# Attention and a silu MLP in one kernel: two vector operations one unit later, and a third of a cast moved to GpSimd

## The chip, the cores and the metric

The kernel runs on one core of a Trainium2 chip. The metric is device time in microseconds of one execution, the median of the runs. All engines of the core work from instruction streams of their own and meet through semaphores: TensorE (PE, with PEld for its weight loads), VectorE (DVE), ScalarE (ACT), GpSimd (POOL), and SyncE (SP), which here issues DMAs.

## The reference

An efficient attention over 8 batches, 8 heads, 576 positions and head dimension 64 gives 4608 tokens of 512 features, and a two-layer MLP with silu follows. Cut to what matters:

```python
def attn(q, k, v):                      # each 8 x 8 x 576 x 64, float32
    q_s = softmax(q, axis=-1)
    k_s = softmax(k, axis=2)            # over the positions
    kv = einsum('bhsd,bhse->bhde', k_s, v)
    return einsum('bhsd,bhde->bhse', q_s, kv)

x = attn(q, k, v).transpose(0, 2, 1, 3).reshape(4608, 512)
h = x @ w_in                            # 512 x 2048
out = (h * sigmoid(h)) @ w_out          # 2048 x 512, float32 out
```

## The kernel before, in words

**Attention, batch by batch.** For a batch, `load` brings q, k and v in two halves each (two pairs of heads, the argument `cc`), in float32, with two buffers for each of the three names. ScalarE takes the exponentials into bf16 (`exp_q`, L108; `exp_k`, L113). VectorE sums q's exponentials (`qsum`, L154 or in two pieces L156, and its reciprocal L158), and `qnorm` (L163) multiplies by it, on VectorE or GpSimd. `vcast` (L91 on VectorE and GpSimd, L89 on ScalarE, both in the helper `copy`) casts v to bf16 into `vaug`, beside a column of constants that gives the sum over k. `kv` (L195) is the small product of k and v, `kvcopy` (L206, L208) its division into `kvn`. The transposed q (by TensorE, L181, for batches 0 and 1, by a DMA transpose, L173, after) times `kvn` gives the tokens: `xt_mm` (L234), whose result is copied to the tile `XT`.

**The MLP, in chunks of tokens.** Chunk 0 is batch 0's 576 tokens; the later ones have 512 columns, the next of them 448 that are new. The first product of chunk 0 runs block by block of 128 features (`wide_mm`, L267; silu as ScalarE's tanh, L256, and VectorE's product, L257). Its second product is plain (`mm2_plain`, L414). From chunk 1 on the products follow a scheme with seven products instead of eight (orders 1, 2, 6, 5, 7, 4, 3). In the first layer, `group` (L377) makes one of the seven: products 1, 6 and 7 are copied from PSUM to `h` (`group_snap`, L89 or L91), and after products 2, 7 and 3 VectorE adds the bank to `h` (`group_add`, L355). The bank of products 2, 5 and 3 is one and the same, so TensorE can't start product 5 before the addition after 2 has read it, nor 3 before the one after 7. Silu reads PSUM or `h` (`group_silu`, L361). The scheme's sums and differences of weights and tokens are VectorE's: `ws_op` (L328), `xs_op` (L338), `t_op` (L461) and, for the second layer, `s_op` (L451). The second layer's products are `prod` (L477); its results are scaled and added by VectorE (L497, L508, and L725 at the end) and stored. Half of chunk 1's first layer is done without the scheme (`mm1`, L285).

**The order of work** is written out by hand: each engine runs its instructions in the order in which the program emits them. The program keeps a list of units, each a group of matmuls with what follows them, and `plan(u, f)` hangs other work in front of unit `u`:

```python
for u, f in enumerate(units):
    for g in at.get(u, ()):
        g()
    f()
```

`begin[1]`, called `b1`, is where the first product of chunk 1 is interleaved with the second of chunk 0. Units b1+0 to b1+8 are plain second products, b1+9 is product 1 of the group, b1+10 plain, b1+11 product 2 with its addition, b1+12 product 6, b1+13 plain, b1+14 product 5. `begin[NCH]` is the unit at which the last chunk's second layer begins; in the 28 units before it the last chunk's first layer alternates with the second layer of the chunk before. There, `s_op(last, 1, 4, 8)` and `s_op(last, 2, 4, 8)` prepare half of two operands of the last chunk's second layer.

**The start.** It isn't in units but emitted in line. SP issues the loads of batch 0 (q, q, k, v, k, v). GpSimd makes a copy of one element that waits for k's first half (`gate`, L569), and issues then, in this order, five loads of `w_in` (L554, cast from float32 to fp16 on the way) and the loads of batch 1 between those of `w_out` (L560): q, q, w_out, k, k, w_out, v, v. TensorE runs fillers on a constant tile (`heat`, L551) where it would stand still: three of them lie before the second `kv` of batch 0. The second cast of v of batch 0 is done in two parts, one pair's head on ScalarE and the other on VectorE.

Of the kernel before, what the change touches and what calls it, by code (L numbers as in the profile page):

```python
# [17 lines left out]
def kernel(  # L18
# [9 lines left out]
    nc = tc.nc  # L28
    B, H, S, D = q.shape
# [3 lines left out]
    J = S // P  # L33
# [7 lines left out]
    NCH = NT // TCH  # L41
# [25 lines left out]
    vaug = glob.tile([128, J, NG, E1], BF16, name="vaug")  # L67
# [19 lines left out]
    def copy(eng, o, i):  # L87
        if eng is nc.scalar:
            eng.copy(out=o, in_=i)  # L89
        else:  # L90
            eng.tensor_copy(o, i)  # L91

    def load(b, name, src, cc, eng):
        t = ld.tile([128, 2, J * D], FP32, name=name)
        st[b][name, cc] = t
        x = src[b].rearrange("(g r) (p j) d -> g (r p) (j d)", r=2, j=J)
        eng.dma_start(out=t, in_=x.rearrange("g x y -> x g y")[:, 2 * cc:2 * cc + 2, :])

    def jgd(b, name, cc):
        return st[b][name, cc].rearrange("p g (j d) -> p j g d", d=D)  # L100

    def half(t, cc):
        return t[:, :, cc * 128:(cc + 1) * 128].rearrange("p j (g d) -> p j g d", d=D)

    def exp_q(b, cc, g0=0, g1=2):
        if "eq" not in st[b]:
            st[b]["eq"] = ap.tile([128, J, NG * D], BF16, name="eq")
        nc.scalar.activation(  # L108
            out=half(st[b]["eq"], cc)[:, :, g0:g1], in_=jgd(b, "qt", cc)[:, :, g0:g1], func=ACT.Exp
        )  # L110
# [1 line left out]
    def exp_k(b, cc):  # L112
        nc.scalar.activation(out=half(ek, cc), in_=jgd(b, "kt", cc), func=ACT.Exp)  # L113

    def vcast(b, cc, eng, g0=0, g1=2):
        o = vaug[:, :, 2 * cc + g0:2 * cc + g1, 0:D]
        i = jgd(b, "vt", cc)[:, :, g0:g1, :]
        copy(eng, o, i)

    def vcast_at(t, b, cc):  # L120

        if t == 2 and cc == 1:
            nc.gpsimd.tensor_copy(gate, SS[2][0:1, 0, 0:1])
        vcast(b, cc, nc.gpsimd)
# [20 lines left out]
    def new_zq(b):  # L145
        if "zq" not in st[b]:
            st[b]["zq"] = ap.tile([128, 2, J, 2], FP32, name="zq", bufs=2)
            st[b]["rzq"] = ap.tile([128, 2, J, 2], FP32, name="rzq", bufs=2)

    def qsum(b, cc, gs=None):  # L150
        new_zq(b)
        z, e = st[b]["zq"][:, cc], half(st[b]["eq"], cc)
        if gs is None:
            nc.vector.reduce_sum(out=z, in_=e, axis=AX.X)  # L154
        else:
            nc.vector.reduce_sum(out=z[:, :, gs], in_=e[:, :, gs, :], axis=AX.X)  # L156
        if gs != 0:
            nc.vector.reciprocal(out=st[b]["rzq"][:, cc], in_=z)  # L158

    def qnorm(b, cc, eng):  # L160
        e = half(st[b]["eq"], cc)
        r = st[b]["rzq"][:, cc]
        eng.tensor_tensor(  # L163
            out=e, in0=e, in1=r[:, :, :, None].to_broadcast([128, J, 2, D]), op=ALU.mult
        )
# [21 lines left out]
    def trcopy(b, cc, j0, j1, bank, eng=nc.vector):  # L187
        t = PS[:, bank, :].bitcast(BF16)[:, 0:(j1 - j0) * 128].rearrange("x (j y) -> x j y", y=128)
        copy(eng, new_qt(b)[:, j0:j1, cc, :], t)
# [249 lines left out]
    def blk(t, kh, th):  # L439
        return GTS[t % 2][:, kh * HF:(kh + 1) * HF, th * HT:(th + 1) * HT]  # L440

    def s_op(t, i, f0=0, f1=HF):
        in0, in1, op = {
            1: (blk(t, 0, 1), blk(t, 1, 1), ALU.add),
            2: (SS[1], blk(t, 0, 0), ALU.subtract),
            3: (blk(t, 0, 0), blk(t, 0, 1), ALU.subtract),
            4: (blk(t, 1, 0), SS[2], ALU.subtract),
        }[i]
        f = slice(f0, f1)
        o = blk(t, 0, 1) if i == 3 else SS[i]  # L450
        nc.vector.tensor_tensor(out=o[:, f], in0=in0[:, f], in1=in1[:, f], op=op)  # L451
# [97 lines left out]
    def heat(n, bank=5):  # L549
        for _ in range(n):  # L550
            nc.tensor.matmul(out=PS[:, bank, :], lhsT=warm[:, 0:128], rhs=warm, start=True, stop=True)  # L551

    def load_w1(f0, f1, c0=0, c1=NC):
        nc.gpsimd.dma_start(  # L554
            out=W1[:, c0:c1, f0 * 128:f1 * 128],
            in_=w_in[c0 * 128:c1 * 128, f0 * 128:f1 * 128].rearrange("(c p) f -> p c f", p=128),
        )
# [14 lines left out]
    load_w1(4, 8)  # L572
    load_w1(8, 12)
    load_w1(12, 16)
    load(1, "qt", q, 0, nc.gpsimd)
    load(1, "qt", q, 1, nc.gpsimd)
    load_w2(0, 4)
# [11 lines left out]
    heat(7)  # L589
    qnorm(0, 1, nc.vector)  # L590
    vcast(0, 0, nc.scalar)
    trcopy(0, 0, 0, 5, 0, nc.scalar)
    trcopy(0, 0, 5, J, 1)
# [5 lines left out]
    xt_mm(0, 0, 0, 320, 4, 0)  # L599
    xt_mm(0, 0, 320, 256, 0, 0)  # L600
    heat(3, 6)
    vcast(0, 1, nc.scalar, 0, 1)
    vcast(0, 1, nc.vector, 1, 2)
    trcopy(0, 1, 0, 5, 2, nc.scalar)
    trcopy(0, 1, 5, J, 3)
    kv(0, 1)
# [16 lines left out]
    def plan(u, f):  # L623
        at.setdefault(u, []).append(f)
# [7 lines left out]
    begin = {1: len(units)}  # L632
# [83 lines left out]
    begin[NCH] = len(units)  # L716
    last = NCH - 1
    plan(begin[NCH] - 11, lambda: s_op(last, 1, 4, 8))
    plan(begin[NCH] - 7, lambda: s_op(last, 2, 4, 8))
    plan(begin[NCH], lambda: (s_op(last, 1, 0, 4), s_op(last, 2, 0, 4), s_op(last, 3)))  # L720
    plan(begin[NCH] + 6, lambda: s_op(last, 4))

# [48 lines left out]
    b1 = begin[1]  # L771
# [26 lines left out]
    plan(b1 + 10, lambda: (xs_op(1, 1), ws_op(1, 0)))  # L798
    plan(b1 + 10, lambda: (xs_op(1, 2), xs_op(1, 3), xs_op(1, 4)))
    plan(b1 + 10, lambda: exp_q(2, 0))  # L800
    plan(b1 + 11, lambda: (qsum(2, 0, 0), qsum(2, 0, 1), qnorm(2, 0, nc.gpsimd)))
    plan(b1 + 13, lambda: exp_q(2, 1))
    plan(b1 + 14, lambda: exp_k(2, 0))
    plan(b1 + 14, lambda: (qsum(2, 1, 0), qsum(2, 1, 1), qnorm(2, 1, nc.gpsimd)))
# [56 lines left out]
```

## Time and profile before

| | |
|---|---|
| median of 11 runs | 263.33 us |
| lowest and highest | 263.04 and 264.27 us |
| the profiled execution | 263.6 us |
| its span in the profile | 261.8 us |
| TensorE busy | 252.2 us, 96% of the span |
| VectorE, ScalarE, GpSimd busy | 209.0, 187.5 and 65.6 us |
| granted TensorE clock, mean | 0.995 |

The profile is of one execution. The span runs from the first to the last instruction of the program; the execution's own time has 1.8 us more around it. All times in the timelines below count from the span's start. Matmuls are pipelined and their ends are modelled, so a matmul's duration is longer than the distance to the next one. A line number stands for the line in the kernel that made the instruction; the helper `copy` gives its own two lines to everything that goes through it. In the chain of work, each step is followed back to what released it.

### The profile page before, as it was taken

To read this page: it belongs to the slowest core of one execution; us is meant where nothing else is said; L and a number is where in the kernel's file an instruction comes from. 1 tells how busy PE (TensorE), PEld (TensorE's weight loads), DVE (VectorE), ACT (ScalarE), POOL (GpSimd) and SP (SyncE) were. 2 spreads that over 40 slices of the span, in tenths; PEclk is the share of its full clock that TensorE was granted. 3 is DMA by queue.
4 is the path that set the end of the run, shared out by engine and by line. 5 is a ranking of instruction groups with operands and counts; after the bars stand their busy time and mean duration, and the time that the engine had idled before them with its cause. 6 is when DMAs were issued, how large, how long until landed. Compare 5 with 4: busy or idle time off the path is not lost.

```text
span 261.8 us, 6409 instructions
## 1 busy us (share of the span) xinstructions
PE 252.2 (96%) x2732; PEld 203.5 (78%) x2732; DVE 209.0 (80%) x268; ACT 187.5 (72%) x212; POOL 65.6 (25%) x63
## 2 busy tenths in 40 slices
PE   8899899799999999999999999999999999999992
PEld 2467656465888888888888888888888888888881
DVE  2867797998997999799979997999798548855832
ACT  4766987798995799579957995799573748484610
POOL 1653791470360306030603060306000000000003
PEclk9999999999999999999999999999999999999997
DMA  7999999669999586957794879540534003300624
GB/s 238 345 185 296 299 314 334 262 106 377 318 341 199 165 221 231 202 145 199 253 223 122 213 241 195 149 92 3 90 75 87 3 0 81 81 3 1 139 64 120
DMA packets 35964, 45.89 MB, mean 175 GB/s; under 512 B 16208, under 2 KB 21008, under 8 KB 35936
## 3 DMA queue, kind: packets, MB, share of 16 engines
q1 hardware_dynamic: 29568, 33.69, 47.5%
q0 software_dynamic: 6128, 11.60, 17.3%
q8 instruction: 21, 0.34, 0.5%
q10 hardware_dynamic: 240, 0.20, 0.2%
q14 instruction: 7, 0.06, 0.1%
HBM read 36.70 MB, written 9.44 MB: 176 GB/s over the span
## 4 chain that ended last, share of the span: by engine, by line
PE 83%; DMA 5%; issue 4%; POOL 2%; ACT 2%; DVE 2%; POOLq 0%; ACTq 0%
PE PS L477 36%; PE PS L377 34%; DMA qt<-in_q_dram 5%; PE PS L414 5%; PE PS L285 2%; PE PS L234 2%; PE PS L195 2%; POOL W L554 1%; PE PS L267 1%; POOL out_dram L740 1%; ACT eq L108 1%; DVE zq L156 1%; ACT sg L256 0%; PE PS L181 0%; DVE h L355 0%
## 5 line engine op out<-in xcount | busy, mean ns | idle before, releaser
L355 DVE TENSOR_TENSOR h<-PS,h 128x1024 f32<-128x1024 f32 (+1 forms) x45 | 53.9, 1198 | 12.2 <-ACT h L89 6.3
L477 PEld LDWEIGHTS <-GT 128*128 128x128 f16 x512 | 49.6, 98 | 6.9 <-issue 1.2
L377 PEld LDWEIGHTS <-WS 128*128 128x128 f16 x480 | 46.8, 98 | 7.9 <-issue 2.3
L477 PE MATMUL PS<-W,GT 128*128 128x256 f16 x384 | 49.1, 273 | 0.0
L377 PE MATMUL PS<-XS,WS 128*128 128x256 f16 (+1 forms) x360 | 46.3, 272 | 1.5 <-DVE h L355 1.5
L361 ACT ACTIVATE GT<-h 128x1024 f16<-128x1024 f32 (+1 forms) x45 | 46.1, 1047 | 0.3 <-DVE h L355 0.3
L89 ACT COPY h<-PS 128x1024 f32<-128x1024 f32 (+1 forms) x35 | 35.1, 1004 | 14.8 <-PE PS L377 14.2
L477 PEld LDWEIGHTS <-S 128*128 128x128 f16 x384 | 37.2, 98 | 5.2 <-issue 1.0
L163 POOL TENSOR_TENSOR eq<-eq,rzq 128x1152 bf16<-128x1152 bf16 x13 | 27.5, 2117 | 54.6 <-DVE rzq L158 51.8
L377 PEld LDWEIGHTS <-W 128*128 128x128 f16 x360 | 34.7, 98 | 4.7 <-issue 0.2
L477 PE MATMUL PS<-T,S 128*128 128x256 f16 x256 | 32.7, 273 | 0.0
L377 PE MATMUL PS<-XT,W 128*128 128x256 f16 (+1 forms) x240 | 29.5, 272 | 0.0
L361 ACT ACTIVATE GT<-PS 128x1024 f16<-128x1024 f32 (+1 forms) x15 | 15.3, 1017 | 18.9 <-PE PS L377 18.9
L91 POOL CAST vaug<-vt 128x1152 bf16<-128x1152 f32 x12 | 14.8, 1242 | 45.2 <-DMA vt<-in_v_dram 45.2
L108 ACT ACTIVATE eq<-qt 128x1152 bf16<-128x1152 f32 (+1 forms) x18 | 19.1, 1059 | 3.5 <-DMA qt<-in_q_dram 3.5
L740 POOL DMA_DIRECT2D out_dram<-ow x5 | 2.7, 546 | 72.5 <-DVE ow L725 72.5
L154 DVE TENSOR_REDUCE zq<-eq 128x18 f32<-128x1152 bf16 x12 | 16.1, 1345 | 4.0 <-ACT eq L108 4.0
L113 ACT ACTIVATE ek<-kt 128x1152 bf16<-128x1152 f32 x16 | 18.4, 1154 | 1.3 <-DMA kt<-in_k_dram 1.3
L267 PE MATMUL PS<-XT,W 128*128 128x288 f16 x128 | 16.0, 286 | 0.8 <-DVE GT L257 0.8
L477 PE MATMUL PS<-W,S 128*128 128x256 f16 x128 | 16.5, 273 | 0.0
L497 DVE SCALAR_TENSOR_TENSOR ow<-PS,sc 128x512 f32<-128x512 f32 x7 | 4.8, 691 | 14.5 <-ACT sc L493 14.5
L267 PEld LDWEIGHTS <-W 128*128 128x128 f16 x128 | 12.4, 98 | 4.3 <-issue 1.2
(79 smaller groups left out, 348.9 us busy)
## 6 DMA issues: line engine op xcount, KB each, us to landing
out_dram<-ow SPq DMA_DIRECT2D x64, 128.0 KB, 2.4
qt<-in_q_dram SPq DMA_DIRECT2D x12, 576.0 KB, 4.7
kt<-in_k_dram SPq DMA_DIRECT2D x12, 576.0 KB, 5.4
vt<-in_v_dram SPq DMA_DIRECT2D x12, 576.0 KB, 6.0
qt<-in_q_dram POOLq DMA_DIRECT2D x4, 576.0 KB, 10.5
kt<-in_k_dram POOLq DMA_DIRECT2D x4, 576.0 KB, 13.6
vt<-in_v_dram POOLq DMA_DIRECT2D x4, 576.0 KB, 12.7
W<-in_moe_w_out_dram POOLq DMA_DIRECT2D x4, 512.0 KB, 14.9
```

What stands on the lines that cost most here:

```text
L89: eng.copy(out=o, in_=i)
L91: eng.tensor_copy(o, i)
L108: nc.scalar.activation(out=half(st[b]["eq"], cc)[:, :, g0:g1], in_=jgd(b, "qt", cc)[:, :, g0:g1], func=ACT.Exp)
L113: nc.scalar.activation(out=half(ek, cc), in_=jgd(b, "kt", cc), func=ACT.Exp)
L154: nc.vector.reduce_sum(out=z, in_=e, axis=AX.X)
L163: eng.tensor_tensor(out=e, in0=e, in1=r[:, :, :, None].to_broadcast([128, J, 2, D]), op=ALU.mult)
L267: nc.tensor.matmul(out=PS[:, WIDE[fb] + n, 0:S // 2], lhsT=W1[:, c, fb * 128:(fb + 1) * 128], rhs=XTS[0][:, c, n * (S // 2):(n + 1) * (S / ...
L355: nc.vector.tensor_tensor(out=four(t, i), in0=group_bank(t, True), in1=four(t, i), op=ALU.add)
L361: nc.scalar.activation(out=group_out(t, f, n), in_=x, func=ACT.Silu, scale=1.0 / XS)
L377: nc.tensor.matmul(out=PS[:, bank + p // 2, (p % 2) * HT:(p % 2) * HT + width(t)], lhsT=a[:, c, p * 128:(p + 1) * 128], rhs=bb[:, c, 0:wid ...
L414: nc.tensor.matmul(out=PS[:, 2 + tb, :], lhsT=GTS[t % 2][:, fc, tb * 128:(tb + 1) * 128], rhs=W2[:, fc, :], start=(fc == 0), stop=(fc == N ...
L477: nc.tensor.matmul(out=PS[:, bank, m * HN:(m + 1) * HN], lhsT=a[:, fc, m * 128:(m + 1) * 128], rhs=bb[:, fc, :], start=(first and fc == 0) ...
```

## The change

Three edits:

- `plan` for the sum of batch 2's first half of q, with its reciprocal and `qnorm`, goes from unit b1+11 to b1+12. On VectorE the addition after product 2 now stands ahead of the sum instead of behind the reciprocal. `qnorm` keeps its place on GpSimd.
- `plan` for `s_op(last, 2, 4, 8)` goes from seven units before `begin[NCH]` to six. On VectorE one addition (L355) now stands ahead of it.
- In the second cast of v of batch 0, the rows of tokens `j` 6 to 8 of both heads go to GpSimd, and ScalarE and VectorE keep rows 0 to 5. On GpSimd, the cast stands behind the five loads of `w_in` and ahead of the loads of batch 1 and `w_out`. TensorE's `kv` waits for it at row 6.

Nothing else changes its order on any engine, and no DMA is added.

```diff
-    def vcast(b, cc, eng, g0=0, g1=2):
-        o = vaug[:, :, 2 * cc + g0:2 * cc + g1, 0:D]
-        i = jgd(b, "vt", cc)[:, :, g0:g1, :]
+    def vcast(b, cc, eng, g0=0, g1=2, j0=0, j1=J):
+        o = vaug[:, j0:j1, 2 * cc + g0:2 * cc + g1, 0:D]
+        i = jgd(b, "vt", cc)[:, j0:j1, g0:g1, :]
         copy(eng, o, i)
...
     load_w1(12, 16)
+    vcast(0, 1, nc.gpsimd, 0, 2, 6, J)
     load(1, "qt", q, 0, nc.gpsimd)
...
     heat(3, 6)
-    vcast(0, 1, nc.scalar, 0, 1)
-    vcast(0, 1, nc.vector, 1, 2)
+    vcast(0, 1, nc.scalar, 0, 1, 0, 6)
+    vcast(0, 1, nc.vector, 1, 2, 0, 6)
...
-    plan(begin[NCH] - 7, lambda: s_op(last, 2, 4, 8))
+    plan(begin[NCH] - 6, lambda: s_op(last, 2, 4, 8))
...
-    plan(b1 + 11, lambda: (qsum(2, 0, 0), qsum(2, 0, 1), qnorm(2, 0, nc.gpsimd)))
+    plan(b1 + 12, lambda: (qsum(2, 0, 0), qsum(2, 0, 1), qnorm(2, 0, nc.gpsimd)))
```

## The prediction

> **What bounds the kernel now.** I read the page first: its busy shares and its chain, for which engine sets the end.
>
> ```profile
> PE 252.2 (96%) x2732; PEld 203.5 (78%) x2732; DVE 209.0 (80%) x268; ACT 187.5 (72%) x212; POOL 65.6 (25%) x63
> ...
> PE 83%; DMA 5%; issue 4%; POOL 2%; ACT 2%; DVE 2%; POOLq 0%; ACTq 0%
> ```
>
> TensorE is busy for 96% and is 83% of the chain. A change pays only where TensorE stands still, so the next view is the list of waits, for TensorE's rows.
>
> ```profile
> PE PS L377 <- DVE h L355: 1.5, 1, 1.5
> ...
> PE PS L267 <- DVE GT L257: 0.8, 1, 0.8
> ```
>
> Two waits matter: 1.5 us on an addition (L355) and 0.8 us on a silu product (L257). I looked up each in the timeline. First the stretch around 46 us (start, duration, instruction; in brackets idle time and what ended it):
>
> ```profile
> 44.10 0.93 PE L377 MATMUL PS<-XT,W 128*128 128x224 f16 x8
> ...
> 45.49 1.41 DVE L156 TENSOR_REDUCE zq<-eq 128x9 f32<-128x576 bf16 x2 [0.98 <-ACT eq L108]
> 45.63 1.03 PE L414 MATMUL PS<-W,GT 128*128 128x512 f16 x4
> ...
> 46.94 0.27 DVE L158 RECIPROCAL rzq<-zq 128x18 f32<-128x18 f32 x1
> 47.12 1.03 DVE L355 TENSOR_TENSOR h<-PS,h 128x896 f32<-128x896 f32 x1
> 47.39 2.11 POOL L163 TENSOR_TENSOR eq<-eq,rzq 128x1152 bf16<-128x1152 bf16 x1 [7.26 <-DVE rzq L158]
> ...
> 48.06 1.98 DVE L328 TENSOR_TENSOR WS<-WS,W 128x1024 f16<-128x1024 f16 x1
> 48.20 0.93 PE L377 MATMUL PS<-XS,WS 128*128 128x224 f16 x8 [1.54 <-DVE h L355]
> ```
>
> The addition's product was ready at 45.03 (44.10 + 0.93). VectorE stood idle then, but its next instruction in order was the sum of batch 2's exponentials (L156), which waited for ScalarE until 45.49. Sum and reciprocal take 1.6 us, and so the addition starts at 47.12 and TensorE resumes at 48.20.
>
> The other wait comes from the start. The chain holds "DMA qt" from 12.59 to 25.74; ScalarE's first exponential of batch 1 waits for it and pushes silu and TensorE:
>
> ```profile
> 12.59 1.48 POOL L97 DMA_DIRECT2D qt<-in_q_dram  x2
> ...
> 25.76 0.68 ACT L108 ACTIVATE eq<-qt 128x576 bf16<-128x576 f32 x1 [0.82 <-DMA qt<-in_q_dram]
> ...
> 28.94 3.10 PE L267 MATMUL PS<-XT,W 128*128 128x288 f16 x24 [0.76 <-DVE GT L257]
> ```
>
> And near the end, TensorE again meets an addition of VectorE's, behind a half-size subtraction (L451):
>
> ```profile
> 240.74 0.69 DVE L451 TENSOR_TENSOR S<-S,GT 128x1024 f16<-128x1024 f16 x1
> 241.35 1.22 DVE L355 TENSOR_TENSOR h<-PS,h 128x1024 f32<-128x1024 f32 x1
> 241.55 1.04 PE L477 MATMUL PS<-W,S 128*128 128x256 f16 x8
> ...
> 242.62 1.03 PE L377 MATMUL PS<-XT,WS 128*128 128x256 f16 x8
> ```
>
> **Part A, the sum of batch 2 one unit later (gain 1.63).** On VectorE only the addition passes ahead of sum and reciprocal; nothing else changes place, and the DMA queues of SP and GpSimd keep their order around it.
> 1. The addition waits for its product (45.03) and a ScalarE copy (over at 44.40), so it runs 45.06 to 46.09. The four matmuls from 45.63 are issued in 0.86, so TensorE can go on at 46.49 instead of 48.20: **1.71** less.
> 2. What is late next? VectorE's own queue gains less. Sum from 46.01, reciprocal at 47.46 (1.45 after the sum's start, as now), L328 at 47.64 (0.18 behind the reciprocal, as the addition now). GpSimd's multiplication (L163) comes 0.45 after the reciprocal starts, at 47.90.
> 3. Now L328 takes 1.98 us where its other seven rows show 0.68 to 0.69. It came at 48.06, with L163 already running, and ended 0.55 after L163's end at 49.49: it stood until GpSimd was done. In the changed order it comes 0.26 *before* L163. Two prices. The row itself, 1.98, is the nearest, but it is of the opposite order. The Trainium skill, "SBUF — State Buffer", section "Who interferes with whom", says that of a VectorE instruction with two SBUF inputs and a GpSimd one that reads SBUF, the first to issue keeps the shared port for all of its length and the other waits. The trace has one case with VectorE ahead: L461 gets the port at 53.93, when L163 ends, and GpSimd's cast, begun at 53.87, takes 2.16 instead of 1.15. So I take 0.68 for L328, and GpSimd's multiplication ends at 50.30 (48.32, plus 2.12, less 0.13 of start that overlapped in that cast). With the row's price the part loses; that is rival 1.
> 4. Then the second sum 48.24 to 49.64, reciprocal 49.67, next addition 50.02 (ScalarE's copy of the group before ends at 49.99), all before TensorE needs them (52.25). Second multiplication 50.25 to 52.36; L461 waits for it and ends 1.08 later at 53.44, as now (53.93 to 55.01); casts of v end at 54.46 and 55.56 instead of 56.03 and 57.13. From here VectorE is **1.57** ahead of before, TensorE 1.71.
> 5. Where the two meet: kvn of batch 2 (L208, ends 59.42 now) at 57.85, and TensorE wants it at 57.83 (59.54 less 1.71). With 0.05 from end to start, it waits some 0.07. Gain left: **1.63**. Loads are no obstacle: k and v of batch 2 land by 51.67 and are wanted at 49.89 (the second k, landed 48.70) and later than 52.3 (v). Behind 60 us TensorE has no wait on VectorE in the list of waits, so the gain goes through to the end. If some cover is gone there, I put it at up to 0.4 less.
>
> **Part B, the half subtraction one unit later (gain 0.20).** The addition then starts as soon as VectorE is free at 240.74 and ends at 241.96. TensorE's eight matmuls from 241.55 are issued in 0.87 (0.109 each), so it goes on at 242.42 instead of 242.62. The subtraction (0.69) falls behind it and ends at 242.6; the store's scaling after it (L508) is at 242.49 either way, and the subtraction's result is read only at 247.86. Cost nothing, cover five microseconds.
>
> **Part C, a third of v's cast on GpSimd (0).** ScalarE's and VectorE's casts of 576 elements (0.67 and 0.76, from 13.00) shrink to 384. ScalarE's rows 0.67 and 1.16 (1152) give 0.51; VectorE's 0.76 scaled by two thirds, with some fixed cost, 0.50 to 0.56. GpSimd's 1152 in 1.15 give 0.4 to 0.5 with its start. All are done by 13.55. TensorE's kv starts at 13.73, but its three fillers from 12.89 hold it until about 13.55: 0.17 at most. The skill speaks against this pairing: "VectorE: DVE Perf Modes", section "Mode 2×_2P — use both read ports for one tensor", lets a copy from SBUF to SBUF take both ports where the outer dimensions are even, or odd and equal. By that rule the present cast (9 rows on both sides) would take about 0.45 (estimate); the trace has 0.76, one element at a time. By the row, 0.17 gained here; by the rule, 6 rows at two elements, VectorE would hold GpSimd off for 0.36 and its third would end near 13.8, about as kv's seventh row wants it: 0.1 gained or lost. Either way it doesn't reach the end, for TensorE stops at 28.0 for the silu that hangs on qt's landing at 25.74, and just waits longer there.
>
> The cast's price is its place in GpSimd's queue: behind the five loads of w_in and ahead of all later ones. It waits for v at 12.98, so q's load is issued at about 13.45 instead of 12.59, **0.86** later, and so the ones behind it up to k's second (16.45, which waited anyway). Bounds: 0.86 lost if q lands as much later, 0 if it is queued. The last w_in load was issued at 11.86 and took 12.4 us to land (24.24); q followed 1.5 us later at 25.74, and the sixteen DMA engines were busy without a break from 12.6 to 25.7 (share 1.17). The queue is full for 10 us past the new issue, so I take 0.
>
> **Sum.** 1.63 + 0.20 + 0 = 1.83. The profiled execution took 263.6 (span 261.8), so 261.77; it stands 0.27 above the median of 263.33. From the median: **261.5 us**, 0.7% faster. A difference within 0.2% (0.53 us) can't be told from none here.
>
> **The rivals.**
> 1. *GpSimd gets the port first* (chance 0.08; slower). If L163 still comes ahead of L328, VectorE stands until 50.01 and is 0.51 later than now from there: L328 ends at 50.56, kvn at 59.93, TensorE starts on it 0.44 later than now, and part A costs 0.44: 263.33 + 0.44 − 0.20 = 263.6. It decides if L163 moves forward by over 0.26 against L328. For: the row of 1.98. Against: L163 starts only after the reciprocal's end and a semaphore, L328 waits for nothing of GpSimd's. A further 0.3 lost behind it would make it slower by over 0.2%.
> 2. *q lands later* (0.06). The wait at 28.94 grows by up to 0.86: 261.5 + 0.86 = 262.4. For: it is on the chain. Against: the full queue.
> 3. *VectorE becomes the bound up to 60 us* (0.14). It is busy nearly throughout from 45.5; if a cast of v or a reduction is stretched, the gain shrinks to between 0.4 and 1.2: 262.1 to 262.9.
> 4. *More than reckoned* (0.05): some slack behind 60 us turns useful, 260.9.
>
> My forecast holds with 0.67. The range is 261.0 to 262.6: it takes in case 2 and most of case 3. Faster by over 0.2%: the forecast, cases 2 and 4 and nearly all of case 3, 0.90. Within 0.2%: most of case 1 and a rest of case 3, 0.06. Slower: 0.04.
>
> **What would show it.** TensorE's wait of 1.54 at 48.2 is gone and its matmuls of L377 begin near 46.5; L328 there takes 0.7 and L163 behind it 2.4 (if 2.0 and 2.1, rival 1); L461 ends near 53.4; the matmuls of L234 now at 59.54 begin near 57.9. At the end the pause before 242.62 is gone. At the start kv begins near 13.6, q is issued near 13.45 and lands near 25.74, and TensorE waits about 0.9 at 28.9. I am wrong if q lands past 26.0, or if a new wait on L208 or on v's casts shows up between 52 and 60 us.

## The result and the profile after

| | before | after |
|---|---|---|
| median, both run on the same chips | 263.65 us (47 runs, 262.73 to 264.6) | 261.56 us (12 runs, 261.13 to 262.5) |
| the profiled execution and its span | 263.6, 261.8 us | 262.03, 260.2 us |

The ratio is 0.9928, with an interval of 0.9916 to 0.994: 0.72% faster, where 0.7% was forecast (261.5 us). The page of the kernel after: its busy shares, its chain, and the group of TensorE's matmuls that used to wait:

```profile
PE 251.2 (97%) x2732; PEld 202.9 (78%) x2732; DVE 207.1 (80%) x268; ACT 187.3 (72%) x212; POOL 66.5 (26%) x64
...
PE 84%; DMA 6%; DVE 4%; POOL 1%; ACT 1%; issue 1%; SPq 0%; POOLq 0%; ACTq 0%
...
L377 PE MATMUL PS<-XS,WS 128*128 128x256 f16 (+1 forms) x360 | 46.3, 272 | 0.0
```

TensorE still sets the end. GpSimd has one instruction more, the cast. In TensorE's list of waits, the row of 1.5 us on the addition (L355) is gone; the last number of the L377 row, the idle time before it, is 0.0. The timeline where it was:

```profile
45.24 1.09 DVE L355 TENSOR_TENSOR h<-PS,h 128x896 f32<-128x896 f32 x1 [0.63 <-PE PS L377]
...
46.25 1.40 DVE L156 TENSOR_REDUCE zq<-eq 128x9 f32<-128x576 bf16 x2
...
46.60 0.93 PE L377 MATMUL PS<-XS,WS 128*128 128x224 f16 x8
...
47.69 0.27 DVE L158 RECIPROCAL rzq<-zq 128x18 f32<-128x18 f32 x1
...
47.87 0.63 DVE L328 TENSOR_TENSOR WS<-WS,W 128x1024 f16<-128x1024 f16 x1
...
48.13 4.41 POOL L163 TENSOR_TENSOR eq<-eq,rzq 128x1152 bf16<-128x1152 bf16 x2 [7.91 <-DVE rzq L158]
...
51.15 2.48 DVE L461 TENSOR_TENSOR T<-W,T 128x2048 f16<-128x2048 f16 x1
...
58.09 0.41 PE L234 MATMUL PS<-qT,kvn 64*64 64x128 bf16 x8
```

The addition now waits for its product and nothing else, the sum follows it, and TensorE's product 5 starts at 46.60 with no idle time in brackets. L328 is ahead of GpSimd's L163 and takes 0.63. The end of the kernel, in the timeline:

```profile
239.18 1.22 DVE L355 TENSOR_TENSOR h<-PS,h 128x1024 f32<-128x1024 f32 x1
...
240.10 1.04 PE L477 MATMUL PS<-W,S 128*128 128x256 f16 x8
...
240.31 0.68 DVE L451 TENSOR_TENSOR S<-S,GT 128x1024 f16<-128x1024 f16 x1
...
240.97 1.04 PE L377 MATMUL PS<-XT,WS 128*128 128x256 f16 x8
```

The addition precedes the half subtraction, and L377 stands 0.87 behind the start of the eight matmuls before it: the pace at which TensorE issues them. The start, around the cast that is now in three parts, and the first load behind it:

```profile
12.92 0.51 ACT L89 CAST vaug<-vt 128x384 bf16<-128x384 f32 x1 [0.16 <-DMA vt<-in_v_dram]
12.92 0.36 DVE L91 CAST vaug<-vt 128x384 bf16<-128x384 f32 x1 [0.47 <-DMA vt<-in_v_dram]
12.95 0.70 POOL L91 CAST vaug<-vt 128x384 bf16<-128x384 f32 x1 [0.34 <-DMA vt<-in_v_dram]
...
13.60 1.45 POOL L97 DMA_DIRECT2D qt<-in_q_dram  x2
...
13.63 0.48 PE L195 MATMUL PS<-vaug,ek 64*64 64x65 bf16 x36
```

GpSimd's 384 elements take twice the time of VectorE's, and q's load waits behind them. What hangs on that load, later in the same timeline:

```profile
25.87 0.68 ACT L108 ACTIVATE eq<-qt 128x576 bf16<-128x576 f32 x1 [0.67 <-DMA qt<-in_q_dram]
...
29.04 0.41 PE L267 MATMUL PS<-XT,W 128*128 128x288 f16 x2 [0.61 <-DVE GT L257]
```

**Where the time came from.** Two stretches between fixed points of TensorE's work, cut from both traces so that a shift of the start doesn't enter. From the start of product 2 of chunk 1 to the first L234 of batch 2: 15.44 us before, 13.88 after, **1.56** less. From the first L377 matmul with 256 columns, at 61.92 after and 63.37 before, to the last L377 group, at 240.97 and 242.62: 179.25 before and 179.06 after, **0.19** less. What comes before the first L414 took 31.91 and takes 32.02: **0.11** more. Together that is 1.64, and the spans differ by 1.6. The medians differ by 2.09, about 0.5 more, since the start is not the same in every execution: in the traces of the other kernels here with the same order of loads, the first L414 comes between 30.8 and 31.6, and the profiled execution after is itself 0.47 above its median.

### The profile page after: what moved, and what is told of

Its sections match the earlier page's. It is cut to its first block, busy times and chain, and to the rows that moved or that the text cites. A ratio compares the mean times of both kernels' runs of the same rounds, so it can differ in the third digit from the quotient of the medians.

```text
span 260.2 us, 6413 instructions
## 1 busy us (share of the span) xinstructions
PE 251.2 (97%) x2732; PEld 202.9 (78%) x2732; DVE 207.1 (80%) x268; ACT 187.3 (72%) x212; POOL 66.5 (26%) x64
## 4 chain that ended last, share of the span: by engine, by line
PE 84%; DMA 6%; DVE 4%; POOL 1%; ACT 1%; issue 1%; SPq 0%; POOLq 0%; ACTq 0%
PE PS L477 37%; PE PS L377 35%; PE PS L414 4%; DMA W<-in_moe_w_in_dram 3%; PE PS L267 3%; DMA kt<-in_k_dram 3%; PE PS L234 2%; PE PS L195 2%; DVE T L461 2%; PE PS L285 1%; POOL out_dram L741 1%; POOL W L554 1%; DVE GT L257 1%; ACT sg L256 0%; DVE h L355 0%
## 5 line engine op out<-in xcount | busy, mean ns | idle before, releaser
L355 DVE TENSOR_TENSOR h<-PS,h 128x1024 f32<-128x1024 f32 (+1 forms) x45 | 54.0, 1199 | 12.8 <-ACT h L89 6.3
L377 PEld LDWEIGHTS <-WS 128*128 128x128 f16 x480 | 46.8, 98 | 6.1 <-issue 0.2
L377 PE MATMUL PS<-XS,WS 128*128 128x256 f16 (+1 forms) x360 | 46.3, 272 | 0.0
L163 POOL TENSOR_TENSOR eq<-eq,rzq 128x1152 bf16<-128x1152 bf16 x13 | 27.7, 2133 | 53.9 <-DVE rzq L158 53.1
L377 PEld LDWEIGHTS <-W 128*128 128x128 f16 x360 | 34.7, 98 | 4.8 <-issue 0.2
L377 PE MATMUL PS<-XT,W 128*128 128x256 f16 (+1 forms) x240 | 29.5, 272 | 0.0
L91 POOL CAST vaug<-vt 128x1152 bf16<-128x1152 f32 (+1 forms) x13 | 15.5, 1198 | 44.4 <-DMA vt<-in_v_dram 32.4
L267 PE MATMUL PS<-XT,W 128*128 128x288 f16 x128 | 16.2, 286 | 0.9 <-DVE GT L257 0.6
L267 PEld LDWEIGHTS <-W 128*128 128x128 f16 x128 | 12.3, 98 | 4.6 <-issue 1.0
```

Of the source, the lines that this page charges most:

```text
L163: eng.tensor_tensor(out=e, in0=e, in1=r[:, :, :, None].to_broadcast([128, J, 2, D]), op=ALU.mult)
L267: nc.tensor.matmul(out=PS[:, WIDE[fb] + n, 0:S // 2], lhsT=W1[:, c, fb * 128:(fb + 1) * 128], rhs=XTS[0][:, c, n * (S // 2):(n + 1) * (S / ...
L355: nc.vector.tensor_tensor(out=four(t, i), in0=group_bank(t, True), in1=four(t, i), op=ALU.add)
L377: nc.tensor.matmul(out=PS[:, bank + p // 2, (p % 2) * HT:(p % 2) * HT + width(t)], lhsT=a[:, c, p * 128:(p + 1) * 128], rhs=bb[:, c, 0:wid ...
```

## The experiments

Each leaves the before kernel as it was but for its edit. The "first stretch" is the one from product 2 of chunk 1 to the first L234 of batch 2, and the "late stretch" the one between the two L377.

**1. Part A alone (a_only).**

```diff
-    plan(b1 + 11, lambda: (qsum(2, 0, 0), qsum(2, 0, 1), qnorm(2, 0, nc.gpsimd)))
+    plan(b1 + 12, lambda: (qsum(2, 0, 0), qsum(2, 0, 1), qnorm(2, 0, nc.gpsimd)))
```

> The kernel before with one edit: the sum of batch 2's first half, its reciprocal and multiplication one unit later. Theory (VectorE's order is what held TensorE at 48 us, and issue order decides the port): 1.5 to 1.65 us faster than before, ratio 0.994; L328 takes about 0.65 and the multiplication on GpSimd 2.3. Rival (the gain of the whole change came from the start or the end): under 0.4 us.

Measured: 261.57 against 263.29 us, ratio 0.9939 (0.9919 to 0.9959). The first stretch takes 13.89: 1.55 less. L328 takes 0.63 and the two L163 4.41 together, as in the kernel after. Part A carries the result.

**2. Part B alone (b_only).**

```diff
-    plan(begin[NCH] - 7, lambda: s_op(last, 2, 4, 8))
+    plan(begin[NCH] - 6, lambda: s_op(last, 2, 4, 8))
```

> The kernel before with one edit: the half subtraction near the end one unit later. Theory (TensorE waited 0.2 us for the addition behind it): 0.2 us faster, ratio 0.9992, at the edge of what five rounds tell; the pause before TensorE's L377 at 242.62 is gone in the trace. Rival (the subtraction, now later, is awaited in its turn): no gain, or a loss of some tenths, with a new wait on L451 behind 244 us.

Measured: 263.06 against 263.29, ratio 0.9997 (0.9987 to 1.0008). The time can't show a gain of 0.2. The trace can: the late stretch takes 179.05 instead of 179.25, and nothing waits for L451.

**3. Part C alone (c_only).**

```diff
     load_w1(12, 16)
+    vcast(0, 1, nc.gpsimd, 0, 2, 6, J)
     load(1, "qt", q, 0, nc.gpsimd)
...
-    vcast(0, 1, nc.scalar, 0, 1)
-    vcast(0, 1, nc.vector, 1, 2)
+    vcast(0, 1, nc.scalar, 0, 1, 0, 6)
+    vcast(0, 1, nc.vector, 1, 2, 0, 6)
```

> The kernel before with one edit: a third of the second cast of v of batch 0 on GpSimd. Theory (TensorE stops at 28 us for q's load in any case, and that load is queued behind w_in): within 0.2 us of before; kv starts 0.1 us earlier; q lands within 0.15 us of before although it is issued 1.0 us later. Rival (q lands as much later as it is issued): 0.9 to 1.0 us slower.

Measured: 263.34 against 263.29, ratio 1.0002 (0.9988 to 1.0016). But the first stretch, 30 us after the cast, takes 15.76 instead of 15.44. Its timeline:

```profile
43.01 0.91 ACT L89 COPY h<-PS 128x896 f32<-128x896 f32 x1 [0.32 <-issue]
...
45.01 1.41 DVE L156 TENSOR_REDUCE zq<-eq 128x9 f32<-128x576 bf16 x2 [1.30 <-ACT eq L108]
...
47.72 0.93 PE L377 MATMUL PS<-XS,WS 128*128 128x224 f16 x8 [1.85 <-DVE h L355]
```

ScalarE stands for 0.32 ahead of its copy to `h` and waits for nothing that the profile shows ("issue"). Its exponential of q comes that much later, so does the sum on VectorE, and in the old order the addition stands behind the sum: TensorE waits 1.85 instead of 1.54. The pause is there in the kernel after too, 0.33 at 43.91, and costs nothing, because the addition no longer stands behind the sum. The prediction had no term for this; experiments 11 and 12 are about its cause.

**4. q's load ahead of the last load of `w_in` (q_early).** Tests whether q lands by when it is issued or by its place in the queue.

```diff
-    load_w1(12, 16)
     load(1, "qt", q, 0, nc.gpsimd)
+    load_w1(12, 16)
```

> The kernel before with one edit: q's first load of batch 1 is issued ahead of the last load of w_in instead of behind it. Theory (loads of one queue land in the order of issue, and q's landing sets TensorE's stop at 28 us): q lands near 23.3 instead of 25.7, the last w_in near 25.7 and still ahead of its use at 27; the stop of 0.9 us at 28 us shrinks to under 0.3: 0.6 to 0.9 us faster. Rival (the stop comes from ScalarE having too much to do there, with q or without): no change.

Measured: 262.72 against 263.29, ratio 0.9982 (0.997 to 0.9994): some 0.5 us, a little under the 0.6 to 0.9 expected. q lands at 22.48 and the last `w_in` at 24.95: they change places in landing too. In the timeline ScalarE no longer waits for q, and TensorE's L267 runs without its stop at 28 us up to the first L414:

```profile
21.78 8.98 PE L267 MATMUL PS<-XT,W 128*128 128x288 f16 x72
...
24.49 0.68 ACT L108 ACTIVATE eq<-qt 128x576 bf16<-128x576 f32 x1
...
30.64 0.59 PE L414 MATMUL PS<-W,GT 128*128 128x512 f16 x2
```

So the place in the queue decides. In the traces of all kernels here, q lands 1.47 to 1.53 behind the load in front of it, whichever load that is. Part C put q 1.01 later into a queue that was full, and it landed 0.11 later; one place further forward, q lands between 22.4 and 22.9 (three kernels) instead of between 24.6 and 25.9 (the others). In two of the others, c_rows7 and act_plus1, q happened to land at 24.6, and TensorE had no stop there either, which fits: q's landing sets the stop.

**5 and 6. Who has the port first (port_vector, port_gpsimd).** Part A with a reduction of 0.7 us more on VectorE, of data that nobody reads: once ahead of the sum, where it delays the reciprocal and all behind it alike, once between reciprocal and L328, so that GpSimd's L163 gets ahead of L328 (rival 1).

```diff
+    def extra():
+        new_zq(2)
+        nc.vector.reduce_sum(out=st[2]["zq"][:, 1, :, 0], in_=st[1]["qT"][:, :, 0, 0:D], axis=AX.X)
 # port_vector:
+    plan(b1 + 12, lambda: (extra(), qsum(2, 0, 0), qsum(2, 0, 1), qnorm(2, 0, nc.gpsimd)))
 # port_gpsimd:
+    plan(b1 + 12, lambda: (qsum(2, 0, 0), qsum(2, 0, 1), extra(), qnorm(2, 0, nc.gpsimd)))
```

> The sum one unit later alone, with one more reduction of 0.74 us on VectorE (its result is overwritten) ahead of the sum. L328 still comes ahead of GpSimd's multiplication. Theory (VectorE's queue sets this stretch, the first to issue keeps the port): everything on VectorE is 0.66 us later than with the edit alone, so 0.8 to 0.95 us faster than before; L328 takes about 0.65. Rival (TensorE has slack here): as fast as with the edit alone.

> The same additional reduction, but between the reciprocal and L328, so that GpSimd's multiplication starts 0.3 to 0.4 us ahead of L328. The work is the same on each engine. Theory (issue order decides who waits): L328 takes about 2.3 us, the multiplication 2.1; VectorE is 1.6 us later than with the reduction ahead of the sum, and the run is 1.3 to 1.6 us slower than that one, 0.5 to 0.8 us slower than before. Rival (the edit's order of issue doesn't matter, or the two share): within 0.4 us of the other.

Measured against 263.0 us: port_vector 262.28, ratio 0.9969 (0.9953 to 0.9985); port_gpsimd 263.74, ratio 1.0027 (1.0011 to 1.0042). The first stretch takes 14.55 and 16.02, against 13.89 for part A alone and 15.44 before. The timeline of port_vector:

```profile
47.82 0.63 DVE L328 TENSOR_TENSOR WS<-WS,W 128x1024 f16<-128x1024 f16 x1
...
48.09 4.41 POOL L163 TENSOR_TENSOR eq<-eq,rzq 128x1152 bf16<-128x1152 bf16 x2 [8.57 <-DVE rzq L158]
```

and that of port_gpsimd:

```profile
47.55 2.11 POOL L163 TENSOR_TENSOR eq<-eq,rzq 128x1152 bf16<-128x1152 bf16 x1 [7.91 <-DVE rzq L158]
...
47.89 2.31 DVE L328 TENSOR_TENSOR WS<-WS,W 128x1024 f16<-128x1024 f16 x1
...
52.83 0.93 PE L377 MATMUL PS<-XT,WS 128*128 128x224 f16 x8 [0.90 <-DVE h L355]
```

The same instructions with the same operands: whichever issues first has its own length, and the other takes its own length and the rest of the first, less some 0.1. With GpSimd ahead, L328 costs 1.68 more (2.31 less 0.63), TensorE waits at the next addition, and the kernel is slower than before. Between these two kernels of the same work lie 1.47. Against part A alone the order costs more, 2.13 (16.02 less 13.89): ahead of the sum, the extra reduction costs 0.66 in the stretch (14.55 less 13.89), but in port_gpsimd it is over at 47.97, and L328 waits for GpSimd until 49.66 with or without it.

**7 and 8. Other splits of the cast (c_rows8, c_rows7).** GpSimd takes one row or two of nine, and ScalarE and VectorE eight or seven.

```diff
+    vcast(0, 1, nc.gpsimd, 0, 2, 8, J)
+    vcast(0, 1, nc.scalar, 0, 1, 0, 8)
+    vcast(0, 1, nc.vector, 1, 2, 0, 8)
 # c_rows7: 7 in place of 8
```

> The cast's edit alone, with 8 rows on VectorE and ScalarE and one on GpSimd. Theory (an even outer dimension lets VectorE take two elements at a time and the shared port with it): VectorE's cast of 512 elements takes about 0.43 us, and GpSimd's cast ends after VectorE's. Rival (the short cast came from GpSimd's taking a share): about 0.68 us.

> The cast's edit alone, with 7 rows on VectorE and ScalarE and two on GpSimd. Theory (an odd outer dimension keeps VectorE at one element at a time and off the shared port): VectorE's cast of 448 elements takes about 0.62 us, longer than that of 8 rows, and GpSimd's cast runs beside it and takes its own 0.3 to 0.4. Rival (odd and even are alike): about 0.39 us.

Each ran once, 263.29 and 262.83 us, which says nothing on so small an effect. The timeline does. Of c_rows8:

```profile
12.63 0.43 DVE L91 CAST vaug<-vt 128x512 bf16<-128x512 f32 x1 [0.35 <-DMA vt<-in_v_dram]
12.66 0.55 POOL L91 CAST vaug<-vt 128x128 bf16<-128x128 f32 x1 [0.22 <-DMA vt<-in_v_dram]
```

and of c_rows7:

```profile
12.36 0.62 DVE L91 CAST vaug<-vt 128x448 bf16<-128x448 f32 x1
12.39 0.40 POOL L91 CAST vaug<-vt 128x256 bf16<-128x256 f32 x1
```

VectorE takes 0.36, 0.43, 0.62 and 0.76 us for 6, 8, 7 and 9 rows: eight rows are quicker than seven. From 6 to 8 rows an element costs 0.5 ns (0.07 for 128), from 7 to 9 it costs 1.1 ns (0.14 for 128): an even number of rows runs at twice the rate of an odd one. The rows are those of the output. In the trace, each of these casts reads v as one run of 384, 512, 448 or 576 elements, because the rows of one pair of heads stand directly behind one another in v's tile, and writes 6, 8, 7 or 9 rows of 64 into `vaug`. And GpSimd takes longer for 128 elements beside the quick cast (0.55) than for 256 beside the slow one (0.40): the quick one holds it off.

**9 and 10. The changed kernel with q early, without and with part C (ab_q_early, all_q_early).** Both have parts A and B and the edit of experiment 4; in all_q_early GpSimd's cast stands behind the last load of `w_in`, so that q's load passes it.

```diff
-    load_w1(12, 16)
     load(1, "qt", q, 0, nc.gpsimd)
+    load_w1(12, 16)
+    vcast(0, 1, nc.gpsimd, 0, 2, 6, J)      # all_q_early alone
```

> The kernel before with the two moves on VectorE and q's first load ahead of the last load of w_in; no cast on GpSimd. Theory (the three gains lie in three places and add): 1.5 + 0.2 + 0.5 = 2.2 us faster than before, 0.3 to 0.6 faster than the changed kernel, ratio 0.991 to 0.992. Rival (what q's early load gains is met again by a later wait, for w_in or for batch 2's loads): as fast as the changed kernel, 1.7 to 1.8 us.

> The same with a third of v's cast on GpSimd as in the changed kernel, behind the last load of w_in. Theory (TensorE at the start is next held by the landing of w_in, so an earlier kv is met by that): within 0.15 us of the kernel without the cast's part. Rival (with the stop at 28 us gone, the 0.1 to 0.17 us of kv come through): 0.1 to 0.2 us faster than it, seen in the trace at the first L414.

Measured against 263.2: ab_q_early 261.14, ratio 0.993 (0.9912 to 0.9948); all_q_early 260.84, ratio 0.9914 (0.9901 to 0.9927). The second has the lowest time of all kernels here. In its timeline TensorE goes through the wide product without a stop:

```profile
17.79 13.03 PE L267 MATMUL PS<-XT,W 128*128 128x288 f16 x105
30.69 0.59 PE L414 MATMUL PS<-W,GT 128*128 128x512 f16 x2
```

Both beat the kernel before. Whether all_q_early beats the changed kernel (0.9914 against 0.9928), and whether part C brings anything in it (0.9914 against 0.993), these runs can't say, since the intervals overlap. For ab_q_early, 2.2 us were expected and 1.7 to 1.8 by the rival; the ratio stands for 1.84 (1.4 to 2.3) and can't tell them apart. In its trace, part of q's gain is lost again on the way: the first L414 comes at 30.87 against 31.30 with part A alone, but product 2 of chunk 1 at 43.36 against 43.49.

**11 and 12. One and four more instructions on ScalarE at the start (act_plus1, act_plus4).** Part C adds one wait on GpSimd to ScalarE's stream, ahead of a cast of v at 37.3 us (c_only), 6 us before the pause. If the pause of experiment 3 comes from where in ScalarE's stream an instruction stands, then any one instruction more should bring it, without a cast on GpSimd, and four should move it elsewhere.

```diff
     nc.scalar.activation(out=dummy, in_=dummy, func=ACT.Exp)
+    nc.scalar.copy(out=dummy, in_=dummy)     # act_plus4: four times
```

> The kernel before with one more copy of a single element on ScalarE at 2 us, where it is idle. Theory (the 0.33 us pause of ScalarE ahead of the first copy to h, seen in all kernels with the cast on GpSimd and in none without, comes from where that copy stands in ScalarE's own instruction stream, which the cast's additional wait shifts by one): the pause is there, the stretch from product 2 of chunk 1 to xt_mm of batch 2 takes 15.76 us instead of 15.44. Rival (the pause is GpSimd's doing: its later queue): no pause, 15.44.

> The same with four such copies. Theory (place in the instruction stream): the pause moves to an earlier instruction of ScalarE, four or so ahead, or is hidden where ScalarE waits anyway; the first copy to h has none, and the stretch takes 15.44 us. Rival (any additional instruction, or GpSimd): a pause at the same copy, or none anywhere.

One run each, 263.51 and 263.34 us. ScalarE's copy in the timeline of act_plus1:

```profile
43.40 0.91 ACT L89 COPY h<-PS 128x896 f32<-128x896 f32 x1 [0.33 <-issue]
```

and of act_plus4:

```profile
43.21 0.91 ACT L89 COPY h<-PS 128x896 f32<-128x896 f32 x1
```

One tiny copy 40 us earlier brings the pause, and the first stretch takes 15.76, as in c_only; with four there is none, and it takes 15.45. The pause stands in the timeline of all six kernels with one instruction more in that stream (c_only, c_rows7, c_rows8, all_q_early, the kernel after, act_plus1) and of none of the others.

The traces also record when each engine takes up its semaphore waits, which the views leave out, and there the pause is in the kernel before as well. It stands ahead of the 64th instruction that the trace records of ScalarE, waits counted, in every kernel where it can be seen. In the kernel before, the 63rd is the copy to `h`, at 43.49, and the 64th the wait that belongs to the next exponential, at 43.83: 0.34 later, but the copy runs for 0.91 and covers it. With one instruction more, the copy itself is the 64th. In c_only it starts 0.37 behind the 63rd, its own wait, with nothing to cover the pause, and the exponential's wait, now the 65th, follows the copy by 0.02. With four more, the 64th is a cast into `XT` at 40.91, for which ScalarE stands idle until TensorE is done anyway, so that no pause can be seen. So the change did not make the pause; it put another instruction behind it. That it hangs on the place in the stream, and not on GpSimd, the port or a DMA that the change moved, is shown; what the engine does in it is not shown.

## Why the prediction was right, point by point

**Part A's steps 1 to 3 held.** The whole trace lies 0.11 later from the start; with that taken off, the addition runs at 45.13 (forecast 45.06), TensorE's product 5 at 46.49 (46.49), L328 0.63 (0.68), L163 begins 0.26 behind it (0.26). The disputed price was right: the row of 1.98 belonged to the opposite order, and the rule that the first to issue keeps the port (the Trainium skill, "SBUF — State Buffer", section "Who interferes with whom") gave the answer that experiments 5 and 6 then measured both ways, 0.63 and 2.31.

**Its steps 4 and 5 were off by 0.07.** The first L163 took 2.33, where 2.40 was reckoned from an earlier start, and the pair ended at 52.54, where 52.36 and the shift of 0.11 give 52.47. L461 and the casts of v behind it, and at last kvn, carry this on: kvn ends at 58.03 (57.85 + 0.11 forecast) and TensorE starts on it at 58.09. The gain was 1.56 instead of 1.63. That VectorE and GpSimd, and no longer TensorE, set the time at this point was part of the working, and so was the size of the margin.

**Part B** was 0.19 to 0.20, as forecast.

**Part C came to about nothing, but two of its terms were mis-sized and one was missing.**
- VectorE's third took 0.36, not 0.50 to 0.56. The term scaled from the row of nine, one element at a time. The other branch, two at a time at six rows and GpSimd held off for 0.36, is what happened: GpSimd's cast ended 0.36 behind VectorE's, and kv started at 13.63, 0.1 earlier than before. The prediction misapplied its rule to the old cast. The rule (the Trainium skill, "VectorE: DVE Perf Modes", section "Mode 2×_2P — use both read ports for one tensor") asks that the outermost counts of input and output be even, or odd and equal, and "9 rows on both sides" is not what the instruction has: its input is one run of 576 and its output nine rows. These counts are neither, so the rule itself gives one element at a time, and the 0.76 agrees. It fits the other three casts too (448 on seven at one element, 512 on eight and 384 on six at two), and read so, it would have given the second branch alone.
- q's load was issued 1.01 later instead of 0.86, mostly because of that hold: it follows the start of GpSimd's cast by 0.65, and by 0.53 in c_rows7, where nothing holds the cast off. It landed 0.11 later; 0 was taken, with 0.86 as the other end. The argument of the full queue stood: q lands some 1.5 us behind the load in front of it (24.38 and 25.85 after, 24.24 and 25.74 before), whenever it was issued, and experiment 4 showed that the place decides.
- The missing term is the pause on ScalarE: part C adds a wait to its stream, and that moved the copy behind the pause. The trace of before had it, though none of its views does. In the old order it costs 0.31, and with part A nothing; that the forecast of 0 held in the whole change is luck in this respect. So the parts do not add: alone they give 1.55 + 0.20 − 0.31 = 1.44 in the stretches, together 1.75. Had part C been made without part A, a forecast of 0 for it would have been 0.31 too good in that stretch.

**The start** ran 0.11 longer: TensorE waited for the third load of `w_in`, which landed at 19.40 instead of 19.12 though it was issued before anything that the change touches. The stop at 28 us was 0.61 instead of 0.76. Such landings differ from execution to execution by more than that (see the spread of the first L414 above), so nothing can be put down to the change here.

**The number.** The gain was 1.83 by forecast, about 1.9 by the ratio (0.72% of 263.65) and 2.09 by the medians. That 261.5 meets 261.56 so closely is in part luck: the median of the kernel before, from which it was reckoned, was 263.33 then and 263.65 in the comparison.

**The rivals.** The first did not occur, and its price was real: port_gpsimd takes 0.58 more than before in the stretch, where 0.44 was reckoned, and the extra reduction is hidden there. The second would have needed a queue with room. The third took 0.07. The fourth found no slack.

## What to carry to other kernels

An in-order engine makes whatever is behind a waiting instruction wait too: put the instruction that the bounding engine needs ahead of one whose input comes later, and then ask what the vacated order does to shared resources, because which of two instructions starts 0.3 us ahead of the other was worth 1.5 to 2.1 us here. A load in a full queue lands by its place and not by its issue, so work may be put ahead of it for nothing while the queue stays full (here for 10 us past the issue), and moving it one place forward may pay more than issuing it earlier. Effects of parts measured alone need not add: a delay counts only through the instruction that waits behind it, and is gone when that instruction is moved.

## What was not expected of the hardware

- A pause of some 0.3 us on ScalarE, with no wait in the profile, stands ahead of the 64th recorded instruction of its stream. A running copy covers it in the kernel before; a single instruction more, 6 us earlier (c_only) or 40 us earlier (act_plus1), uncovers it, and four (act_plus4) do not.
- VectorE casts into eight rows of 64 (0.43 us) quicker than into seven (0.62 us), float32 to bf16, though the input is one run in both.
- A quick cast on VectorE holds a GpSimd cast off: 384 elements took 0.70 us on GpSimd beside VectorE's 0.36, and 256 took 0.40 beside one that ran one element at a time.
